# Two block sums of w2 made in DRAM by transfers, low sums on VectorE, and a wide seventh product

## The chip, the cores and the metric

The kernel runs on one core of a Trainium2 chip. The metric is the device time of one execution in microseconds (us); the time before is the median of three runs. The engines are named as in the profile: PE is TensorE (PEld its weight loads), DVE is VectorE, ACT is ScalarE, POOL is GpSimd and SP is SyncE, which here only issues transfers. L12 is line 12 of the kernel.

## The reference

The reference is one block with two residual parts, in float32. The input x has 2048 tokens of 512 channels.

```python
x = A_x                                       # (1, 2048, 512)
h = x + A_ref(layernorm(x), wqkv, w_phi, wo)  # linear attention, 32 heads of 16
h2 = h + B_ref(layernorm(h), w1, b1, w2, b2)  # MLP across the tokens
...
# A_ref: pq, pk = q @ w_phi, k @ w_phi;  phi = [softmax(p), softmax(-p)]
#        o = phi_q (phi_k^T v) / (phi_q sum(phi_k) + 1e-6);  o @ wo
# B_ref: u = gelu(h^T w1 + b1)   (512 channels x 2048 tokens, w1 2048 x 1792)
#        y = u w2 + b2           (w2 1792 x 2048), transposed back
```

## The kernel before

Each float32 operand is split into a high part and a low part (`split`: ScalarE copies the high part, VectorE or GpSimd subtracts it for the low part), and a product is made from three matmuls: high by high, high by low, low by high.

The work runs in stages. The first pass (0 to 138 us) makes k, v and q of the 16 token tiles and the sums of the linear attention. In before a scheduler orders the engines in this pass except TensorE, whose order is written out (`PASSES`). From there the order of every engine is written out by hand. The second pass (138 to 263 us) has 18 turns of a loop over `it`: `s_ez` and `s_pq` weight the query features on GpSimd, `s_tr` transposes them on TensorE, `s_num` and `s_wo` make the attention output, `s_h` adds it to x, `s_moments`, `s_rstd` and `s_hn` make the layernorm, and `fill` makes the first products with w1 (weights `whl`, loaded by `stream`). Then come the steps with w1 (263 to 372 us) and the steps with w2 (372 to 511 us).

The w2 steps (kind "y") use a seven-product scheme for 2 x 2 blocks. There are 8 block columns `sp` of 256 tokens and 7 steps `p` in each. In one step, `load_raw` puts four 128 x 128 blocks of w2 into slots 1 to 4 of a tile of seven (`wraw`), one transfer per step on SP's queue. Four sums complete them. `w_sums` makes these on VectorE for four steps at once (L793 to L797):

```python
nc.vector.tensor_add(raw[:, :, 0], raw[:, :, 3], raw[:, :, 1])   # L793
nc.vector.tensor_add(raw[:, :, 5], raw[:, :, 0], raw[:, :, 2])   # L794
nc.vector.tensor_add(raw[:, :, 6], raw[:, :, 4], raw[:, :, 5])   # L795
nc.vector.tensor_add(raw[:, :, 1], raw[:, :, 1], raw[:, :, 2])   # L797
```

`w_parts` splits the seven blocks into `wp` (L66 on ScalarE, L67 on VectorE). `prepare` calls both several steps ahead of the products. `wide_step` makes the seven products P1 to P7 in the first seven block columns, `last_step` in the eighth. A product is either `narrow` (three matmuls of 256 columns, L951) or `wide` (one of 512 columns with the high and low part of u side by side, L958, and one of 256 columns with the low weights, L960). A wide product fills both halves of its PSUM bank: the second half holds the sum of high by low, which must be added in the end. Before, P2 to P5 are wide and P1, P6, P7 narrow. The banks are b16 (P1 and P6), b7, b5, b4, b3 and b2. At the end of a block column ScalarE and VectorE combine the banks into four output tiles and add b2, and `store` sends them by adding transfers on GpSimd's queue (L1001) into the output, which holds h. Four stores per block column are made, two of 128 x 512 and two of 128 x 256: the low sums of P4 and of P3 and P2 go as stores of their own.

For the "u" steps with w1, `add_raw` makes sums in the same tile by adding transfers on GpSimd's queue (L783), 128 rows of 1 KB each.

Of the kernel before, what the change touches and what calls it, by code (L numbers as in the profile page):

```python
# [17 lines left out]
P = 128  # L18
# [5 lines left out]
NPR = 2 * NG  # L24
Q_EARLY = 6

PASSES = [(s[0], int(s[1:] or 0)) for s in
          "k5 v f k6 v q k7 q v k8 v q v q k9 k10 v k11 q k12 v k13 v q k14 v".split()]
PKS = 8
SUMS = 8  # L30
Q_TURNS = ((0, 1), (0, 1), (0, 1), (0, 1), (0,), (1,), (0,), (1,))
# [11 lines left out]
def block_kernel(ctx: ExitStack, tc: tile.TileContext, x, xT, wT, phic, wo, w1, b1, w2, b2,  # L43
# [2 lines left out]

    cst = ctx.enter_context(tc.tile_pool(name="cst", bufs=1))
    big = ctx.enter_context(tc.tile_pool(name="big", bufs=NT + 2))

    ident = cst.tile([P, P], F32, name="ident")  # L50
    mask = cst.tile([P, 64], F32, name="mask")
# [62 lines left out]
    def load_h(t):  # L114
        XH[t] = kk.tile([P, D], F32, name="xh", bufs=3)
        nc.sync.dma_start(XH[t], x[t * P:(t + 1) * P, :])

    def split_x(t, raw, alone=False):
# [4 lines left out]
        else:  # L123
            split(X[t][:, 0], X[t][:, 1], raw, nc.gpsimd)

    def stats_x(t):
        junk = kk.tile([P, D], F32, name="sqj", bufs=1)
        st = kk.tile([P, 2], F32, name="st")
        nc.scalar.activation(junk, XH[t], AF.Copy, scale=-1.0 / D, accum_out=st[:, 0:1])
        nc.scalar.activation(junk, XH[t], AF.Square, bias=st[:, 0:1], accum_out=st[:, 1:2])  # L130
        ve = kk.tile([P, 1], F32, name="ve")
        nc.vector.tensor_scalar(ve, st[:, 1:2], 1.0 / D, EPS, op0=ALU.mult, op1=ALU.add)
        nc.gpsimd.tensor_tensor(r1[:, t:t + 1], ve, mhalf[:, :1], op=ALU.pow)

    def proj(t, wh, wl, pool, name, by_part=False, halves=1):
        o = pool.tile([P, D], F32, name=name, tag=name)
# [24 lines left out]
    def logit_ops(src, e, pool):  # L161

        v = src.rearrange("p (j h d) -> p j h d", h=2, d=DH)
        ev = signs(e)
        mx = wk.tile([P, NPR, 2], F32, name="mx")
        mn = wk.tile([P, NPR, 2], F32, name="mn")

        def shift():
            nc.vector.tensor_sub(ev[:, :, 0], v, mx.unsqueeze(3).to_broadcast([P, NPR, 2, DH]))
            if pool:  # L170
                MN.append((ev, mx, mn))
            else:
# [17 lines left out]
    def run(*lists):  # L190
        for op in turns(*lists):
            op()

    def exps(t, e):
        nc.scalar.activation(e, e, AF.Exp, scale=r1[:, t:t + 1])  # L195

    def heads(e):
        return e.rearrange("p g (a d) -> p (g a) d", d=DH)

    def k_ops(t, o):  # L200
        PK[t] = kk.tile([P, NG, P], F32, name="pk", bufs=PKS)
        run(logit_ops(o, PK[t], False))

    def k_logits(t):
        k_ops(t, proj(t, wkh, wkl, ps_k, "pk_ps"))
        exps(t, PK[t])

    def v_out(t, o):
        VS[t] = kk.tile([P, D], F32, name="vs", bufs=5)
        nc.scalar.activation(VS[t], o, AF.Copy, scale=r1[:, t:t + 1])  # L210

    def v_proj(t):
        v_out(t, proj(t, wvh, wvl, ps_v, "pv"))

    def k_norm(t, z=True):
        sk = wk.tile([P, 2 * H], F32, name="sk", bufs=2)
        nc.vector.reduce_sum(sk, heads(PK[t]), axis=AX.X)
        nc.vector.reciprocal(sk, sk)  # L218
        nc.gpsimd.tensor_mul(heads(PK[t]), heads(PK[t]), sk.unsqueeze(2).to_broadcast([P, 2 * H, DH]))  # L219
        if z and t == 0:  # L220
            nc.gpsimd.tensor_copy(zacc, PK[t])
        elif z:
            nc.gpsimd.tensor_add(zacc, zacc, PK[t])  # L223
# [57 lines left out]
    with tc.tile_pool(name="prep", bufs=1) as prep:  # L281
# [77 lines left out]
        with tc.manual_schedule(engines={ET.PE, ET.DVE, ET.Activation, ET.Pool}):  # L359
# [61 lines left out]
            lo_w(0)  # L421
            lo_w(1)
            center(3, False)
        stats_x(3)
        exps(3, PK[3])
        load_h(4)
        stats_x(4)
        k_ops(4, k4)
        exps(4, PK[4])
        v_out(2, v2)  # L430

        def fold_rest():
            for c in range(2, 4):
                fold(c, ps_q, "pu")
                hi_w(c)
                lo_w(c)

        def k_step(t):

            if t + 2 < NT:  # L440
                raw = load_x(t + 2)
                load_h(t + 2)
            if t > 4:
                k_logits(t)
            k_norm(t - 1)
            if t + 2 < NT:
                split_x(t + 2, raw)
                stats_x(t + 2)

        def q_step(_):  # L450
            q_mm()
            run(q_logits(0))
            q_exp(0)
            run(q_sums(0))


        with tc.manual_schedule(engines={ET.PE}):
            k_step(3)
            k_step(4)
            for name, n in PASSES:  # L460
                {"k": k_step, "v": lambda _: v_kv(), "q": q_step, "f": lambda _: fold_rest()}[name](n)

    ms = ExitStack()
    ms.enter_context(tc.manual_schedule(engines={ET.PE, ET.DVE, ET.Activation, ET.Pool, ET.SP}))
# [86 lines left out]
    proj_part(pv, v, wvh, wvl, range(1, KD))  # L551
    v_out(v, pv)
    v += 1
    s_ez(0)
    s_ez(1)
    run(s_den(0, ps_d, "dn"))
# [108 lines left out]
            nc.scalar.activation(HN[t][:, 0], hn, AF.Copy)  # L665
            DL.append(lambda: nc.vector.tensor_sub(HN[t][:, 1], hn, HN[t][:, 0]))

    w1v = w1.rearrange("(k p) f -> p k f", p=P)
    w2v = w2.rearrange("(k p) s -> p k s", p=P)

    COMING, LATER = [], []

    def his():
# [85 lines left out]
    def load_raw(g):  # L759
        if 2 * g >= len(STEPS):  # L760
            return
        b = g // 2 % 2
        if b not in BLOCK:
            BLOCK[b] = cbb.tile([P, 4, 7, P], F32, name="wraw") if b else wqp.tile([P, 4, 7, P], F32, name="wraw", tag="wq")
        RAW[g] = BLOCK[b][:, g % 2 * 2:g % 2 * 2 + 2]
        for k in range(2):
            src, r, c = blocks(2 * g + k)
# [18 lines left out]
    def w_sums(g):  # L786

        if 2 * g >= len(STEPS) or STEPS[2 * g][0] == "v":
            return
        plain = STEPS[2 * g][0] == "y"  # L790
        raw = BLOCK[g // 2 % 2] if plain else RAW[g]
        if plain:
            nc.vector.tensor_add(raw[:, :, 0], raw[:, :, 3], raw[:, :, 1])  # L793
# [35 lines left out]
    for it in range(NT + 2):  # L829
        if it < NT:  # L830
            s_x(it)
        shifted = q["logits"] - len(MN)
        ql = q_logits(0)
        work = turn(it)
# [168 lines left out]
    def wide_step(n, sp, p):  # L1003
# [7 lines left out]
        def x(m):  # L1011
            return UB[p, m]
# [1 line left out]
        def ws_(*products):  # L1014
            wide(n, x, first, end, *products)

        w3, w2, w5, w4 = (b3, P3), (b2, P2), (b5, P5), (b4, P4)
# [12 lines left out]
        ws_(w3, w2)  # L1030
        tmp, ot, lows = [ur.tile([P, 4, HD], F32, name="u") for _ in range(3)]
# [8 lines left out]
        sub(u2, b16[:, 1], e1)  # L1040
# [4 lines left out]
        add(l5, b5[:, 0], l5)  # L1045
        add(e0, l5, u2)
        nc.scalar.activation(lows[:, 0], b3[:, 1], AF.Copy)  # L1047
        nc.scalar.activation(lows[:, 1], b2[:, 1], AF.Copy)
        tile_sum(0, 0, l5, u3)
        tile_sum(1, 0, b3[:, 0], e0, ALU.subtract)  # L1050
        tile_sum(1, 1, b2[:, 0], e1)
        return [(t, 1, lows[:, 3:4]), (t, 0, ot[:, 0:2]), (t + 1, 0, ot[:, 2:4]), (t + 1, 0, lows[:, 0:2])]

    def last_step(n, sp, p):
        t = 2 * sp
# [93 lines left out]
        at(n, u_parts, p)  # L1149
    at(len(STEPS) - 18, last_h, NT - 2)  # L1150
    at(len(STEPS) - 12, last_b, NT - 2)
    HB = []
    load_raw(2)
    load_raw(3)
# [103 lines left out]
```

## Time and profile before

| | before |
|---|---|
| median of 3 runs | 517.14 us (516.28 to 517.21) |
| the profiled execution | 516.23 us, its span 514.454 us |
| granted TensorE clock | 1.000 |
| PE busy | 509.4 us, 99% of the span |
| DVE, ACT, POOL busy | 432.5, 300.7, 247.1 us (84%, 58%, 48%) |
| chain that ended last | PE 95%, DVE 2%, ACT 1% |
| bytes moved | 61.76 MB, mean 120 GB/s |

The span is what the trace covers; the rest of an execution's time lies around it. A share of busy time is a mean over stages with different limits. Matmul times in the rows are times in flight, and the matmuls overlap. A row of the timeline reads: start, duration, engine, line, operation, output<-input, shapes, count, and in brackets the idle time before it and what ended that. A row of groups ends with busy time, mean ns of one, and idle time with its releasers. A row of windows has the busy time of PE, PEld, DVE, ACT and POOL with their counts, then the granted clock, the share of the DMA engines and GB/s.

### The profile page before, as it was taken

What the parts mean: (1) busy time and instruction counts of PE and PEld (TensorE: products, weight loads), DVE (VectorE), ACT (ScalarE), POOL (GpSimd) and SP (SyncE); (2) the same over time, 40 slices, a digit from 0 to 9 for tenths busy, and PEclk for the clock granted to TensorE, in tenths of its full rate; (3) what the DMA queues carried; (4) which work ended last, traced back from release to release, by engine and by line L of the source; (5) the groups of instructions that cost most, each with busy time, mean ns of one, the idle gap of its engine ahead of it and who ended that gap; (6) DMA issues with size and microseconds to landing.
All of it is one profiled execution on the core that took longest, in us unless ns stands there. A gap on an engine that the chain in (4) does not pass through costs nothing.

```text
span 514.5 us, 10292 instructions
## 1 busy us (share of the span) xinstructions
PE 509.4 (99%) x3954; PEld 439.7 (85%) x3954; DVE 432.5 (84%) x736; ACT 300.7 (58%) x530; POOL 247.1 (48%) x195
## 2 busy tenths in 40 slices
PE   9999999999999999999999999999999999999997
PEld 8888888888877777777788999988899999999997
DVE  6799889989887899699876878986789989968973
ACT  6999853526267878867675636555364434434530
POOL 3579997876999999975203330000002112211220
PEclk9999999999999999999999999999999999999999
DMA  8642301020113233443329784333425687668743
GB/s 306 218 143 84 103 22 42 1 77 8 43 62 103 81 104 126 147 160 126 103 79 256 152 194 120 103 103 102 143 63 126 162 194 172 128 152 192 168 63 71
DMA packets 52112, 61.76 MB, mean 120 GB/s; under 512 B 4704, under 2 KB 38752, under 8 KB 52064
## 3 DMA queue, kind: packets, MB, share of 16 engines
q1 hardware_dynamic: 45440, 52.43, 32.6%
q0 software_dynamic: 6336, 8.52, 12.1%
q8 instruction: 31, 0.51, 0.4%
q10 hardware_dynamic: 288, 0.17, 0.1%
q14 instruction: 17, 0.14, 0.1%
HBM read 49.96 MB, written 11.14 MB: 119 GB/s over the span
## 4 chain that ended last, share of the span: by engine, by line
PE 95%; DVE 2%; ACT 1%; issue 0%; DVEq 0%
PE py L951 22%; PE pu L71 10%; PE pu L72 9%; PE pu L73 9%; PE py L958 9%; PE py L960 4%; PE pk_ps L71 3%; PE pk_ps L72 3%; PE pk_ps L73 3%; PE pv L73 3%; PE pv L72 3%; PE pv L71 3%; PE po L71 3%; PE po L73 2%; PE po L72 2%; PE pn L616 2%
## 5 line engine op out<-in xcount | busy, mean ns | idle before, releaser
L66 ACT ACTIVATE wp<-wraw 128x896 fp32r<-128x896 f32 (+1 forms) x96 | 79.8, 869 | 83.4 <-DVE wraw L797 34.1
L67 DVE TENSOR_TENSOR wp<-wraw,wp 128x896 fp32r<-128x896 f32 (+1 forms) x96 | 92.3, 986 | 20.7 <-ACT wp L66 20.5
L1001 POOL DMA_DIRECT2D out<-u x28 | 24.5, 952 | 170.0 <-ACT u L1047 110.8
L951 PE MATMUL py<-cb,wp 128*128 128x256 f32 x582 | 79.8, 283 | 0.0
L951 PEld LDWEIGHTS py<-cb,wp 128*128 128x128 f32 x582 | 74.0, 191 | 0.0
L490 POOL TENSOR_TENSOR ez<-eq,zB 128x1024 f32<-128x1024 f32 x16 | 38.4, 2404 | 3.8 <-ACT zB L550 3.8
L71 PE MATMUL pu<-hs,wp 128*128 128x512 f32 x96 | 37.4, 389 | 0.0
L72 PE MATMUL pu<-hs,wp 128*128 128x512 f32 x96 | 37.4, 389 | 0.0
L73 PE MATMUL pu<-hs,wp 128*128 128x512 f32 x96 | 37.3, 389 | 0.0
L219 POOL TENSOR_TENSOR pk<-pk,sk 128x1024 f32<-128x1024 f32 x16 | 31.1, 1943 | 11.3 <-DVE sk L218 10.1
L958 PE MATMUL py<-cb,wp 128*128 128x512 f32 x126 | 36.1, 394 | 0.0
L514 POOL TENSOR_TENSOR eq<-eq,w 128x1024 f32<-128x1024 f32 x16 | 32.4, 2026 | 3.5 <-DVE w L511 3.5
L223 POOL TENSOR_TENSOR zacc<-zacc,pk 128x1024 f32<-128x1024 f32 x13 | 31.3, 2406 | 0.5
L783 POOL DMA_DIRECT2D wraw<-in_w x16 | 14.2, 970 | 31.7 <-DMA wraw<-in_w 21.3
L195 ACT ACTIVATE pk<-pk,r 128x1024 f32<-128x1024 f32 x16 | 18.4, 1148 | 15.0 <-DVE pk L173 14.4
L951 PE MATMUL py<-uf,wp 128*128 128x256 f32 x198 | 26.6, 283 | 0.0
L71 PE MATMUL pu<-wq,xs 128*128 128x512 f32 x64 | 26.1, 408 | 0.0
L71 PE MATMUL pu<-hs,whl 128*128 128x512 f32 x64 | 26.0, 406 | 0.0
L71 PE MATMUL po<-woh,oh 128*128 128x512 f32 x64 | 25.3, 395 | 0.1
L72 PE MATMUL pu<-wq,xs 128*128 128x512 f32 x64 | 25.0, 391 | 0.0
L72 PE MATMUL pu<-hs,whl 128*128 128x512 f32 x64 | 25.0, 390 | 0.0
L73 PE MATMUL po<-woh,ol 128*128 128x512 f32 x64 | 25.0, 390 | 0.0
(213 smaller groups left out, 1398.5 us busy)
## 6 DMA issues: line engine op xcount, KB each, us to landing
wraw<-in_w SPq DMA_DIRECT2D x112, 256.0 KB, 3.4
out<-u POOLq DMA_DIRECT2D x21, 256.0 KB, 5.2
xraw<-in_xT SPq DMA_DIRECT2D x16, 256.0 KB, 3.0
xh<-in_x SPq DMA_DIRECT2D x16, 256.0 KB, 2.6
h<-in_x SPq DMA_DIRECT2D x16, 256.0 KB, 2.8
out<-h SPq DMA_DIRECT2D x16, 256.0 KB, 2.0
wraw<-in_wT SPq DMA_DIRECT2D x12, 256.0 KB, 5.2
wraw<-in_w POOLq DMA_DIRECT2D x16, 128.0 KB, 3.9
```

The costliest lines, as they stand in the source:

```text
L66: nc.scalar.activation(hi, src, AF.Copy)
L67: lo_engine.tensor_sub(lo, src, hi)
L71: nc.tensor.matmul(o, ah, bh, start=first, stop=False)
L72: nc.tensor.matmul(o, ah, bl, start=False, stop=False)
L73: return nc.tensor.matmul(o, al, bh, start=False, stop=last).ins
L219: nc.gpsimd.tensor_mul(heads(PK[t]), heads(PK[t]), sk.unsqueeze(2).to_broadcast([P, 2 * H, DH]))
L223: nc.gpsimd.tensor_add(zacc, zacc, PK[t])
L490: nc.gpsimd.tensor_mul(EZ[t], EQ[t], zB)
L514: nc.gpsimd.tensor_mul(heads(EQ[t]), heads(EQ[t]), W[t].rearrange("p g c h -> p (g c h)").unsqueeze(2).to_broadcast([P, 2 * H, DH]))
L951: nc.tensor.matmul(o, w[:, m[0]], x[:, y], start=opens and i == 0, stop=closes and i == 2, skip_group_check=True)
L958: nc.tensor.matmul(o, wh_[:, m[0]], x(m[1]), start=first, stop=False, skip_group_check=True)
L1001: nc.gpsimd.dma_start(out[t * P:(t + 1) * P, k * HD:], flat(a), accum_op=ALU.add)
```

## The change

Slots 0 and 1 of a w2 step (the sums of L793 and L797) are made in DRAM. A new DRAM tile `w2s` per block column holds both for all seven steps. `copy_w2(n)` copies one of the two summands on ScalarE's queue, 16 copies of 896 rows of 512 bytes; `add_w2(sp)` adds the other summands by one adding transfer on GpSimd's queue, 8 of 896 rows of 1 KB. The first pass now follows a written order for all engines (`FIRST`), which is the order that the scheduler gave before, with twelve copies and four adds put into it. Adds 4 and 5 stand before the first `s_ez`, adds 6 and 7 in turns 15 and 16 of the second pass, and four copies in its turns 2 to 8. `load_raw` of a w2 step has three transfers: the two sums, one block alone, and two blocks. `w_sums` loses two of its four adds.

In `wide_step` P7 becomes wide. At the end of a block column ScalarE copies one low sum more, VectorE adds the four low sums (four operations more), and two stores of 128 x 512 remain. TensorE's order is otherwise that of before: the built program has 3353 matmuls where it had 3402, 49 fewer.

```diff
+    def copy_w2(n):
+        sp, k = divmod(n, 2)
+        if k == 0:
+            W2S[sp] = dram.tile([P, NP, 2, P], F32, name=f"w2s{sp}")
+        src = w2v.rearrange("p (j i) s -> p j i s", i=2)
+        nc.scalar.dma_start(W2S[sp][:, :, k], src[:, :, 1 - k, 2 * sp * P:2 * sp * P + P])
+
+    def add_w2(sp):
+        src = w2v.rearrange("p (j i) s -> p j i s", i=2)
+        nc.gpsimd.dma_start(W2S[sp].rearrange("p j k s -> p j (k s)"), src[:, :, 0, 2 * sp * P:2 * sp * P + 2 * P],
+                            accum_op=ALU.add)
...
+        with tc.manual_schedule(engines={ET.PE, ET.DVE, ET.Activation, ET.Pool, ET.SP}):
+            for token in FIRST.split():
+                DO[token[0]](int(token[1:]))
...
     v_out(v, pv)
     v += 1
+    add_w2(4)
+    add_w2(5)
     s_ez(0)
...
+            if kind == "y":
+                nc.sync.dma_start(RAW[g][:, k, 0:2], W2S[i][:, j])
+                nc.sync.dma_start(RAW[g][:, k, 2], src[:, r, c + P:c + 2 * P])
+                nc.sync.dma_start(RAW[g][:, k, 3:5].rearrange("p i s -> p (i s)"), src[:, r + 1, c:c + 2 * P])
+                continue
...
-        if plain:
-            nc.vector.tensor_add(raw[:, :, 0], raw[:, :, 3], raw[:, :, 1])
         nc.vector.tensor_add(raw[:, :, 5], raw[:, :, 0], raw[:, :, 2])
         nc.vector.tensor_add(raw[:, :, 6], raw[:, :, 4], raw[:, :, 5])
-        if plain:
-            nc.vector.tensor_add(raw[:, :, 1], raw[:, :, 1], raw[:, :, 2])
...
+        for n in {2: (12,), 4: (13,), 6: (14,), 8: (15,)}.get(it, ()):
+            copy_w2(n)
...
+        if it in {15: 6, 16: 7}:
+            add_w2({15: 6, 16: 7}[it])
...
-            ws_(w3, w2, w5, w4)
+            ws_(w3, w2, w5, w4, w7)
         narrow(b16[:, 0], n, P1, x(1), first, end)
         narrow(b16[:, 1], n, P6, x(5), False, end)
-        narrow(b7[:, 0], n, P7, x(0), first, end)
         if first:
-            ws_(w5, w4)
+            ws_(w7, w5, w4)
         if not end:
             return []
+        ws_(w7)
         ws_(w4, w5)
         ws_(w3, w2)
...
-        nc.scalar.activation(e1, b16[:, 0], AF.Copy)
+        l7, l3, l2, l4 = lows[:, 3], lows[:, 0], lows[:, 1], ot[:, 1]
+        for o, bank in ((e1, b16), (l7, b7), (l5, b5), (l4, b4)):
+            nc.scalar.activation(o, bank[:, int(o is not e1)], AF.Copy)
         sub(u2, b16[:, 1], e1)
         sub(u3, u2, b7[:, 0])
-        nc.scalar.activation(l5, b5[:, 1], AF.Copy)
-        nc.scalar.activation(lows[:, 3], b4[:, 1], AF.Copy)
-        tile_sum(0, 1, b4[:, 0], u3)
         add(l5, b5[:, 0], l5)
+        sub(u3, u3, l7)
+        add(l4, b4[:, 0], l4)
         add(e0, l5, u2)
-        nc.scalar.activation(lows[:, 0], b3[:, 1], AF.Copy)
-        nc.scalar.activation(lows[:, 1], b2[:, 1], AF.Copy)
+        nc.scalar.activation(l3, b3[:, 1], AF.Copy)
+        nc.scalar.activation(l2, b2[:, 1], AF.Copy)
+        tile_sum(0, 1, l4, u3)
         tile_sum(0, 0, l5, u3)
-        tile_sum(1, 0, b3[:, 0], e0, ALU.subtract)
-        tile_sum(1, 1, b2[:, 0], e1)
-        return [(t, 1, lows[:, 3:4]), (t, 0, ot[:, 0:2]), (t + 1, 0, ot[:, 2:4]), (t + 1, 0, lows[:, 0:2])]
+        add(l3, b3[:, 0], l3)
+        add(l2, b2[:, 0], l2)
+        tile_sum(1, 0, l3, e0, ALU.subtract)
+        tile_sum(1, 1, l2, e1)
+        return [(t, 0, ot[:, 0:2]), (t + 1, 0, ot[:, 2:4])]
```

More of the change, by code (lines that the diff above doesn't have):

```diff
@@ L25 @@
 Q_EARLY = 6
-PASSES = [(s[0], int(s[1:] or 0)) for s in
-          "k5 v f k6 v q k7 q v k8 v q v q k9 k10 v k11 q k12 v k13 v q k14 v".split()]
+FIRST = """
+X5 H4 X6 a5 X7 b5 a6 b6 H5 X8 X9 s3 a7 S3 b7 a8 H6 X10 u3 b8 l4 r3 s4 m4 n2 k5 S4 C0 o2 H7 X11 x4 y4 s5 N2 v3
+u4 p2 e3 l5 r4 S5 m5 F2 H8 n3 s6 F3 x5 e4 k6 u5 C1 y5 r5 S6 N3 o3 H9 n4 p3 c2 v4 u6 s7 N4 c3 d2 z2 e5 d3 l6 S7
+C2 K0 m6 K1 H10 r6 s8 n5 K2 p4 S8 K3 o4 H11 q0 x6 u7 y6 s9 C3 z3 u8 e6 N5 k7 S9 n6 H12 s10 r7 N6 r8 S10 u9 p5
+H13 s11 C4 u10 f0 q1 S11 g0 H14 h0 s12 z4 a9 i0 S12 C5 l7 v5 E0 H15 m7 p6 x7 j0 k8 r9 y7 r10 f1 e7 b9 g1 a10
+u11 u12 z5 X12 h1 v6 s13 C6 i1 o5 n7 S13 E1 r11 N7 r12 q2 u13 l8 s14 C7 b10 m8 S14 j1 z6 X13 s15 S15 v7 x8 o6
+y8 p7 u14 e8 C8 q3 o7 n8 r13 r14 f2 z7 g2 k9 u15 N8 h2 i2 r15 p8 f3 E2 C9 k10 g3 a11 C10 j2 a12 z8 a13 C11 h3
+v8 i3 l9 E3 b11 m9 x9 X14 b12 K4 y9 K5 j3 e9 X15 b13 A0 A1 K6 K7 k11 o8 l10 m10 n9 q4 x10 y10 N9 e10 p9 n10
+k12 N10 z9 l11 m11 v9 x11 p10 y11 f4 e11 g4 k13 a14 z10 h4 a15 i4 n11 E4 b14 v10 o9 l12 m12 b15 N11 j4 p11 q5
+x12 y12 z11 l13 e12 k14 m13 x13 y13 n12 e13 v11 o10 N12 n13 p12 f5 g5 z12 N13 h5 i5 p13 l14 E5 m14 o11 x14 z13
+A2 A3 y14 j5 e14
+"""
 PKS = 8
@@ L124, in split_x, with stats_sum, stats_square, stats_var @@
             split(X[t][:, 0], X[t][:, 1], raw, nc.gpsimd)
-    def stats_x(t):
[L127 to L133, printed above, removed]
+    def stats_sum(t):
+        junk = kk.tile([P, D], F32, name="sqj", bufs=1)
+        ST[t] = kk.tile([P, 2], F32, name="st")
+        nc.scalar.activation(junk, XH[t], AF.Copy, scale=-1.0 / D, accum_out=ST[t][:, 0:1])
+    def stats_square(t):
+        junk = kk.tile([P, D], F32, name="sqj", bufs=1)
+        nc.scalar.activation(junk, XH[t], AF.Square, bias=ST[t][:, 0:1], accum_out=ST[t][:, 1:2])
+    def stats_var(t):
+        ST[t], st = kk.tile([P, 1], F32, name="ve"), ST[t]
+        nc.vector.tensor_scalar(ST[t], st[:, 1:2], 1.0 / D, EPS, op0=ALU.mult, op1=ALU.add)
+    def stats_rstd(t):
+        nc.gpsimd.tensor_tensor(r1[:, t:t + 1], ST[t], mhalf[:, :1], op=ALU.pow)
+    def stats_x(t):
+        for f in (stats_sum, stats_square, stats_var, stats_rstd):
+            f(t)
     def proj(t, wh, wl, pool, name, by_part=False, halves=1):
@@ L198, in heads, with logit_list @@
         return e.rearrange("p g (a d) -> p (g a) d", d=DH)
+    def logit_list(t, o):
+        PK[t] = kk.tile([P, NG, P], F32, name="pk", bufs=PKS)
+        return logit_ops(o, PK[t], False)
     def k_ops(t, o):
[L201 to L206, printed above, removed]
+        run(logit_list(t, o))
     def v_out(t, o):
@@ L213, in v_proj, with norm_sum, norm_rec, norm_mul @@
         v_out(t, proj(t, wvh, wvl, ps_v, "pv"))
-    def k_norm(t, z=True):
[L216 to L223, printed above, removed]
+    def norm_sum(t):
+        SK[t] = wk.tile([P, 2 * H], F32, name="sk", bufs=2)
+        nc.vector.reduce_sum(SK[t], heads(PK[t]), axis=AX.X)
+    def norm_rec(t):
+        nc.vector.reciprocal(SK[t], SK[t])
+    def norm_mul(t):
+        nc.gpsimd.tensor_mul(heads(PK[t]), heads(PK[t]), SK[t].unsqueeze(2).to_broadcast([P, 2 * H, DH]))
+    def norm_z(t):
+        if t == 0:
+            nc.gpsimd.tensor_copy(zacc, PK[t])
+        else:
+            nc.gpsimd.tensor_add(zacc, zacc, PK[t])
+    def k_norm(t, z=True):
+        norm_sum(t)
+        norm_rec(t)
+        norm_mul(t)
+        if z:
+            norm_z(t)
     def kv(t):
@@ L423, in block_kernel @@
             center(3, False)
[L424 to L448, printed above, removed]
@@ L450, in q_step, with k_mm @@
-        def q_step(_):
-            q_mm()
[L452 to L461, printed above, removed]
+        LO_K, LO_Q, PV = {4: logit_list(4, k4)}, {}, {2: v2}
+        def k_mm(t):
+            LO_K[t] = logit_list(t, proj(t, wkh, wkl, ps_k, "pk_ps"))
@@ new lines, in v_mm, with q_list, hi_x @@
+        def v_mm(t):
+            PV[t] = proj(t, wvh, wvl, ps_v, "pv")
+        def q_list(n):
+            q_mm()
+            EQ[n] = big.tile([P, NG, P], F32, name="eq", tag="big")
+            LO_Q[n] = logit_ops(PS[n], EQ[n], False)
+        def hi_x(t):
+            X[t] = big.tile([P, 2, KD, P], F32R, name="xs", tag="big")
+            nc.scalar.activation(X[t][:, 0], xr[t], AF.Copy)
+        DO = {
+            "X": lambda t: xr.update({t: load_x(t)}), "H": load_h,
+            "a": hi_x, "b": lambda t: nc.gpsimd.tensor_sub(X[t][:, 1], xr[t], X[t][:, 0]),
+            "s": stats_sum, "S": stats_square, "u": stats_var, "r": stats_rstd,
+            "k": k_mm, "l": lambda t: LO_K[t][0](), "m": lambda t: LO_K[t][1](),
+            "x": lambda t: LO_K[t][2](), "y": lambda t: LO_K[t][3](), "e": lambda t: exps(t, PK[t]),
+            "n": norm_sum, "N": norm_rec, "p": norm_mul, "z": norm_z,
+            "v": v_mm, "o": lambda t: v_out(t, PV[t]), "K": kv,
+            "C": copy_w2, "A": add_w2, "q": q_list, "f": lambda t: LO_Q[t][0](), "g": lambda t: LO_Q[t][1](),
+            "h": lambda t: LO_Q[t][2](), "i": lambda t: LO_Q[t][3](), "E": lambda t: exps(t, EQ[t]),
+            "j": lambda t: run(q_sum(t)), "F": lambda c: fold(c, ps_q, "pu"), "c": hi_w, "d": lo_w,
+        }
@@ L1151, in block_kernel @@
     at(len(STEPS) - 12, last_b, NT - 2)
+    for sp, n in ():
+        at(n, add_w2, sp)
     HB = []
```

19 lines of the change are left out of this document (12 added, 7 removed).

## The prediction

> **What bounds the kernel now.** I read the page first, for its engine shares and the chain that ended last, then TensorE's waits.
>
> ```profile
> span 514.5 us, 10292 instructions
> PE 509.4 (99%) x3954; PEld 439.7 (85%) x3954; DVE 432.5 (84%) x736; ACT 300.7 (58%) x530; POOL 247.1 (48%) x195
> ...
> DMA  8642301020113233443329784333425687668743
> ...
> q1 hardware_dynamic: 45440, 52.43, 32.6%
> q0 software_dynamic: 6336, 8.52, 12.1%
> ...
> PE 95%; DVE 2%; ACT 1%; issue 0%; DVEq 0%
> ```
> ```profile
> PE pk_ps L358 <- DVE eps L62: 1.1, 1, 1.1
> PE pn L616 <- DVE h L641: 0.2, 1, 0.2
> PE pu L336 <- POOL ph L361: 0.2, 1, 0.2
> ```
>
> TensorE (PE) holds 95% of the chain and waits 1.5 us in all, 1.1 of it at the start. So only two things move the time: fewer TensorE cycles, or a new wait of TensorE. Work taken from VectorE, or from the stores on GpSimd (POOL), is worth nothing by itself. The profiled execution took 516.23 us, 1.7 outside its 514.5 span, and lies 0.91 below the median of 517.14. I sum differences against that execution and add them to the median. A difference within 0.2%, 1.03 us, can't be told from none here.
>
> **TensorE's saving.** Forty-nine times (seven block columns by seven steps) the seventh product turns from three 256-column matmuls into one of 512 and one of 256. The chain in order of time prices both forms, inside one w2 step:
>
> ```profile
> 393.41 1.08 PE py L951 x9
> 394.49 0.93 PE py L958 x4
> 395.42 0.47 PE py L960 x4
> ```
>
> Nine narrow ones in 1.08 are 0.120 each, the wide ones 0.2325, their low halves 0.1175. Three narrow are 0.360; one wide and one low 0.350. The saving is 0.010 x 49 = 0.49 us. The rows of groups seem to promise more:
>
> ```profile
> L951 PE MATMUL py<-cb,wp 128*128 128x256 f32 x390 | 54.1, 282 | 0.0
> ...
> L958 PE MATMUL py<-cb,wp 128*128 128x512 f32 x126 | 36.1, 394 | 0.0
> ...
> L960 PE MATMUL py<-cb,wp 128*128 128x256 f32 x126 | 21.5, 279 | 0.0
> ```
>
> 3 x 282 against 394 + 279 would be 173 ns, 8.5 us over 49. But these are times in flight, of matmuls that overlap: 282 ns each, started every 120. I take the chain.
>
> **Adding transfers on GpSimd.** Eight are issued, each 896 rows of 1 KB, DRAM to DRAM, which the trace does not show. Nearest are the adding transfers for w1 of 128 such rows, and the gaps where the new ones stand (two after the low part of x, at 85.36 - 3.17 = 82.2, two before the one at 114.64, two before the first ez at 126.79, one before the rstd at 255.60, one behind it):
>
> ```profile
> L783 POOL DMA_DIRECT2D wraw<-in_w x16: 858/870/1223, 273.4 to 308.8; - x16
> ```
> ```profile
> 85.36 1.94 POOL L219 TENSOR_TENSOR pk<-pk,sk 128x1024 f32<-128x1024 f32 x1 [3.17 <-DVE sk L218]
> ...
> 102.24 1.94 POOL L219 TENSOR_TENSOR pk<-pk,sk 128x1024 f32<-128x1024 f32 x1 [1.20 <-ACT vs L210]
> ...
> 114.64 1.94 POOL L219 TENSOR_TENSOR pk<-pk,sk 128x1024 f32<-128x1024 f32 x1 [3.61 <-DVE sk L218]
> ...
> 126.79 4.75 POOL L490 TENSOR_TENSOR ez<-eq,zB 128x1024 f32<-128x1024 f32 x2 [3.82 <-ACT zB L550]
> ...
> 137.61 1.94 POOL L514 TENSOR_TENSOR eq<-eq,w 128x1024 f32<-128x1024 f32 x1
> ...
> 255.60 0.55 POOL L652 TENSOR_TENSOR r<-ve,mhalf 128x1 f32<-128x1 f32 x1 [2.42 <-ACT ve L649]
> ```
> ```profile
> 142.53 0.28 PE L598 MATMUL tr<-ident,eq 64*128 64x64 f32 x2
> ```
> ```profile
> 131.00:220.00 89.00, 88.78 (x982) 69.74 (x981) 75.82 (x155) 64.43 (x126) 87.00 (x64) 1.00 0.31 101
> ```
>
> Let one issue cost a: at least 0.87 (the median), at most seven times that, 6.1. The three pairs make GpSimd late by max(0, 2a - 3.17); that, less 1.2 of idle time between (the row at 102.2), plus 2a - 3.61; that plus 2a - 3.82. Behind the last pair stand ez and the weighting of the queries (L514), with GpSimd full until 220 (87.00 of 89.00 us in the window), so lateness stays. TensorE takes the second weighting's result at 142.53, and it ends at 139.55, so 3.0 us are covered. At a = 2.0 the pairs end 0.6 late at most, at 2.5 about 3.2, which costs TensorE 0.15 us; from there each 0.1 costs about 0.6. The point of decision is a = 2.5 (2.7 for a loss that can be measured). The gap of 2.42 at 255.60 asks about the same. I take a = 1.5, an estimate nearer the low end: half of the 16 issues lie between 858 and 870 ns, so constant that most of it looks like a fixed part. Price nothing, cover 3.0.
>
> [...] No row here shows more than 128 rows.
>
> **Copies on ScalarE (ACT).** Sixteen of 896 rows of 512 B. A 128-row load occupies its queue 0.34 to 0.43 us (SP's rows below); seven times the larger is 3.0. I take 0.6, since the issue is by hardware and a load of twice as many rows costs little more. Where ScalarE has no idle time to spare, two copies precede the last weights of q:
>
> ```profile
> 43.86 1.22 DVE L354 TENSOR_TENSOR wq<-pu,wq 128x512 fp32r<-128x512 f32 x2
> ```
> ```profile
> 49.15 0.50 PE L71 MATMUL pu<-wq,xs 128*128 128x512 f32 x1
> ```
>
> VectorE is done at 45.08, TensorE asks at 49.15: 4.1 us cover for 1.2; at 3.0 each, 6.0 would cost 1.9. Later copies stand further ahead of what TensorE asks for, the last four where ScalarE waits for VectorE. Price nothing, bound 1.9.
>
> **Packets of the new transfers.** q0's mean packet costs 0.121 x 16 x 514.5 / 6336 = 157 ns, q1's 59. An adding transfer is then 896 x 157 / 16 = 8.8 us of all 16 engines; by bytes, 0.92 of 8.52 MB, it is 6.7. In the first pass the DMA engines are mostly free. Not so for the two at 253 and 256:
>
> ```profile
> 254.53 0.43 SPq L691 DMA_DIRECT2D wraw<-in_w  x1
> ```
> ```profile
> 257.89 0.62 ACT L677 ACTIVATE whl<-wraw 128x512 fp32r<-128x512 f32 x1
> ```
> ```profile
> 258.54 0.69 DVE L684 TENSOR_TENSOR whl<-wraw,whl 128x512 fp32r<-128x512 f32 x1 [1.81 <-ACT whl L677]
> ...
> 260.35 0.68 DVE L666 TENSOR_TENSOR hs<-hf,hs 128x512 fp32r<-128x512 f32 x1
> ```
> ```profile
> 261.25 0.40 PE L72 MATMUL pu<-hs,whl 128*128 128x512 f32 x1
> ```
>
> The w1 load issued at 254.53 is used by ScalarE at 257.89; VectorE waits for that, does two parts, then the low part of hs, done at 261.03 for a matmul at 261.25: 0.2 us of slack. How long that load and the w1 loads from 265 to 300 take from issue to landing:
>
> ```profile
> DMA to landing us min/median/max: 2.8/2.8/2.8
> ```
> ```profile
> DMA to landing us min/median/max: 2.7/3.7/4.9
> ```
>
> It lands at 257.3 and lies 0.6 us before ScalarE is free. The sixth add's packets run from about 255 on and share the engines with it. The later loads share them with adds for w1 and take up to 4.9, so this one comes 0 to 2.1 late, and TensorE stalls by what exceeds 0.8: 0 to 1.3. I take 1.0 late, 0.2 stalled. The seventh add falls on the loads of the w1 steps, before a stretch already full:
>
> ```profile
> 260.00:265.00 5.00, 5.00 (x24) 4.10 (x23) 4.39 (x10) 3.22 (x8) 0.64 (x1) 1.00 0.14 52
> 265.00:270.00 5.00, 5.00 (x24) 4.14 (x23) 3.88 (x5) 4.34 (x7) 0.00 (x0) 1.00 0.50 145
> 270.00:275.00 5.00, 5.00 (x24) 4.14 (x23) 2.39 (x3) 1.14 (x3) 1.56 (x2) 1.00 1.07 355
> ```
>
> From 263 to 270 about 4.2 of 7 us are free, for 6.7 to 8.8: a backlog of 2.5 to 4.6 us behind 270. VectorE idles 4.3 of the 15 us from 260 to 275 (15 less 4.39, 3.88 and 2.39), which absorbs about all of it. I take nothing; the larger backlog against half of that idle time leaves 2.4, my bound.
>
> **The w2 steps.** VectorE loses two adds per four steps and gains four small operations per block; GpSimd's stores go from four to two; a step's load becomes three. Rows:
>
> ```profile
> L793 DVE TENSOR_TENSOR wraw<-wraw 128x512 f32<-128x512 f32 x13 | 8.9, 687 | 5.8 <-DMA wraw<-in_w 5.2 <-DVE wp L67 0.6
> ```
> ```profile
> 389.06 0.42 DVE L1040 TENSOR_TENSOR u<-py,u 128x256 f32<-128x256 f32 x1
> ...
> 390.55 0.41 DVE L1045 TENSOR_TENSOR u<-py,u 128x256 f32<-128x256 f32 x1
> ```
> ```profile
> 389.39 0.63 PE L958 MATMUL py<-cb,wp 128*128 128x512 f32 x2
> ```
>
> Per block VectorE sheds 3.5 x 0.69 = 2.4 and gains 4 x 0.42 = 1.7 us. Two more issues of 0.43 land a load 0.9 later; VectorE already waits 5.2 us for loads here (L793's row) and TensorE does not notice, so 0.9 is covered. What is new is when the banks of b5 and b4 come free: b4's after five operations, not three. At their spacing of 0.50, from 389.06, the fifth ends at 391.47. TensorE wants that bank 1.88 after the block's start at 389.39 (two wide and two low products 0.70, six narrow 0.72, two wide 0.47): 391.27. That is 0.2 late for a start like this one; VectorE, with 0.7 us less per block, starts earlier. Price 0.0, bound 7 x 0.2 = 1.4.
>
> **Sum.** -0.49 + 0.2 = -0.3: 515.9 for the profiled execution, 516.85 on the median, told as 516.9.
>
> **Rivals.**
> *GpSimd's issues cost more than 2.5 us* (slower). By rows in place of transfers, a may be anything to 6.1. At 3.0 the stall is 3.2 us, giving 519.8; at 3.5, 6.2 and 522.8; at 6.1, some 22 and 538. Against it: the flat 0.87. The rows' own spread, 858 to 1223, shows that an issue can be held by others. [...] Chance 0.20, a tenth of all beyond 523.
> *The load at 254.53 comes late and the seventh add holds the w1 loads too* (slower): it decides from 2.4 late on (1.6 stalled, less 0.5 saved). With both bounds, 1.3 + 2.4 = 3.7 stalled, 518.2 to 520.4. For it: the 0.2 slack, and windows with the DMA full. Against it: the load is nearly through when the add's packets come. Chance 0.15.
> *The w2 steps lose their cover* (slower): banks 0.2 to 0.4 late in seven blocks and three small loads for one: 1.5 to 2.8 stalled, 518.2 to 519.5. Chance 0.10.
> *TensorE gains more than the chain says* (faster): if a narrow product's weight load were what paces it, one start of 0.120 fewer each would be 5.9 us, 511.3; by the rows in flight, 508.7. Against it: wide and low products already run in these steps at 0.35 together. A smaller gain, just below 516.1, would come if the seventh product's saving were twice the chain's. That the change does not do what it says is no case: the built program holds 49 matmuls fewer. Chance 0.15.
>
> **How the numbers follow.** Forecast 0.40, within 1.03 of the median before: same 0.40. The three slower rivals sum to 0.45, the faster one to 0.15. The forecast's own range is 516.6 (no stall) to 518.2 (1.5 stalled, where the slower rivals begin). The range given, 515.8 to 523.0, leaves out about a tenth at each end.
>
> **What would show it.** Right: TensorE still with 95% of the chain and the seventh product's pair at 0.35 us; the new issues on GpSimd under 2.5 us each, ez at 126.8, the whl row near 258 and no wait of TensorE above 1 us after the first. Wrong: issue rows of several us and ez past 130; a TensorE wait for hs near 261; waits for banks at block starts; or w2 steps well under 2.46 us.

## The result and the profile after

The changed kernel takes 548.9 us (548.35 to 550.31, five runs) against 516.52 before (516.28 to 517.21, five runs): a ratio of 1.0625 [1.0607, 1.0643]. It is 32 us slower. The forecast was 516.9, in a range up to 523.0. GpSimd's issues were among the rivals, but as too dear in themselves, which they are not, and a time beyond 523 had a chance of a tenth. Adds and copies are numbered from 0 here, as in the change: add 6 is the one that the prediction calls the sixth.

The page of after, profiled in an execution of 548.96 us:

```profile
span 547.2 us, 10409 instructions
...
PE 518.9 (95%) x3905; PEld 443.2 (81%) x3905; DVE 423.1 (77%) x736; ACT 303.2 (55%) x537; POOL 245.9 (45%) x189
...
PEclk9999999997779999999997999999999999999999
...
PE 47%; DVE 3%; DMA 2%; issue 1%; ACT 0%; SPq 0%; DVEq 0%
...
w2s<-in_w ACTq DMA_DIRECT2D x16, 448.0 KB, 5.0
w2s<-in_w POOLq DMA_DIRECT2D x8, 896.0 KB, 9.8
```

TensorE is 9.5 us longer busy with 49 matmuls fewer, and its granted clock falls in two places. Its waits in after, longest first:

```profile
PE pk_ps L595 <- ACT zh L580: 11.6, 1, 11.6
PE pu L98 <- ACT whl L723: 3.1, 1, 3.1
PE tr L647 <- POOL eq L561: 3.0, 1, 3.0
PE pu L98 <- DVE eq L207: 2.4, 1, 2.4
PE pu L99 <- DVE hs L715: 2.0, 1, 2.0
PE pk_ps L409 <- DVE eps L89: 1.1, 1, 1.1
PE pk_ps L596 <- DVE zl L583: 0.6, 1, 0.6
PE po L98 <- DVE ol L674: 0.4, 1, 0.4
```

TensorE's order is the same in both programs up to the w2 steps, so the same matmul can be looked up in both. In before:

```profile
124.97 0.39 PE L548 MATMUL pk_ps<-zh,ones_r 128*128 128x512 f32 x1
...
141.94 0.67 PE L616 MATMUL pn<-pht,small 64*32 64x128 f32 x32
...
263.75 0.39 PE L71 MATMUL pu<-hs,wp 128*128 128x512 f32 x1
```

And in after:

```profile
137.77 0.80 PE L595 MATMUL pk_ps<-zh,ones_r 128*128 128x512 f32 x1 [11.62 <-ACT zh L580]
...
166.25 0.54 PE L665 MATMUL pn<-pht,small 64*32 64x128 f32 x14
...
296.28 0.39 PE L98 MATMUL pu<-hs,wp 128*128 128x512 f32 x1
```

After is 12.8 us behind at the first, 24.3 at the second and 32.5 at the third, and 32.7 at the end of the span. All but the first 1.0 (by 105 us) arises in two places: from 125 to 166 us, and around the last w1 load of the second pass. The w2 steps add nothing and take nothing.

GpSimd's timeline in after shows the first place:

```profile
82.93 1.64 POOL L74 DMA_DIRECT2D w2s<-in_w  x1
92.84 1.49 POOL L74 DMA_DIRECT2D w2s<-in_w  x1 [8.27 <-DVE eq L207]
93.61 2.69 POOL L261 TENSOR_TENSOR pk<-pk,sk 128x1024 f32<-128x1024 f32 x1
...
118.69 1.49 POOL L74 DMA_DIRECT2D w2s<-in_w  x1
128.55 1.49 POOL L74 DMA_DIRECT2D w2s<-in_w  x1 [8.36 <-issue]
129.29 2.71 POOL L261 TENSOR_TENSOR pk<-pk,sk 128x1024 f32<-128x1024 f32 x1
132.08 2.34 POOL L567 TENSOR_TENSOR zacc<-zacc,pk 128x1024 f32<-128x1024 f32 x1
...
138.53 1.51 POOL L74 DMA_DIRECT2D w2s<-in_w  x1 [0.56 <-issue]
148.18 1.48 POOL L74 DMA_DIRECT2D w2s<-in_w  x1 [8.13 <-issue]
148.92 3.15 POOL L537 TENSOR_TENSOR ez<-eq,zB 128x1024 f32<-128x1024 f32 x1
```

An issue itself takes 1.5 us, just what I took for a. But the second of a pair starts 9.6 to 9.9 us after the first, which is how long an add takes to land (9.8 in the page). In the trace's DMA events the first of each pair landed at 92.58, 128.23 and 147.86, and the second starts 0.3 us after that. GpSimd stands idle for 8 us in between. The name behind the arrow does not tell the cause: "DVE eq" ended at 92.59, but an add from DRAM to DRAM reads nothing of it, and the other two have "issue" there. What GpSimd does next is late: the last part of the sum z (132.08, in before 116.66), then `zh`, for which TensorE waits 11.6 us, then ez (148.92, in before 126.79). The row of z in before:

```profile
116.66 2.73 POOL L520 TENSOR_TENSOR zacc<-zacc,pk 128x1024 f32<-128x1024 f32 x1
```

### The profile page after: what moved, and what is told of

Its sections match the earlier page's. It is cut to its first block, busy times and chain, and to the rows that moved or that the text cites. A ratio compares the mean times of both kernels' runs of the same rounds, so it can differ in the third digit from the quotient of the medians.

```text
span 547.2 us, 10409 instructions
## 1 busy us (share of the span) xinstructions
PE 518.9 (95%) x3905; PEld 443.2 (81%) x3905; DVE 423.1 (77%) x736; ACT 303.2 (55%) x537; POOL 245.9 (45%) x189
## 4 chain that ended last, share of the span: by engine, by line
PE 47%; DVE 3%; DMA 2%; issue 1%; ACT 0%; SPq 0%; DVEq 0%
PE py L1003 17%; PE py L1010 10%; PE py L1012 5%; PE pu L99 5%; PE pu L100 5%; PE pu L98 5%; DMA wraw<-in_w 2%; DVE u L785 1%; DVE whl L730 1%; DVE u L784 0%; DVE ol L674 0%; PE po L98 0%; DVE tr L550 0%; DVE wp L94 0%; ACT pht L649 0%
## 5 line engine op out<-in xcount | busy, mean ns | idle before, releaser
L1053 POOL DMA_DIRECT2D out<-u x14 | 12.0, 859 | 177.6 <-DVE u L1104 173.4
L1003 PE MATMUL py<-cb,wp 128*128 128x256 f32 x477 | 66.1, 283 | 0.0
L1003 PEld LDWEIGHTS py<-cb,wp 128*128 128x128 f32 x477 | 61.1, 192 | 0.0
L1010 PE MATMUL py<-cb,wp 128*128 128x512 f32 x161 | 45.3, 394 | 0.0
L261 POOL TENSOR_TENSOR pk<-pk,sk 128x1024 f32<-128x1024 f32 x16 | 32.6, 2039 | 3.4 <-DVE sk L258 3.4
L1010 PEld LDWEIGHTS py<-cb,wp 128*128 128x128 f32 x161 | 27.6, 189 | 3.4
L98 PE MATMUL pu<-hs,whl 128*128 128x512 f32 x64 | 26.8, 418 | 3.1 <-ACT whl L723 3.1
L98 PE MATMUL pu<-wq,xs 128*128 128x512 f32 x64 | 27.2, 425 | 2.4 <-DVE eq L207 2.4
L1012 PEld LDWEIGHTS py<-cb,wp 128*128 128x128 f32 x161 | 25.4, 189 | 3.6
L99 PE MATMUL pu<-hs,whl 128*128 128x512 f32 x64 | 26.1, 408 | 2.0 <-DVE hs L715 2.0
L234 ACT ACTIVATE eq<-eq,r 128x1024 f32<-128x1024 f32 x16 | 18.4, 1150 | 17.2 <-DVE eq L212 8.9
L74 POOL DMA_DIRECT2D w2s<-in_w x8 | 12.1, 1518 | 34.1 <-issue 25.9
```

What stands on the lines that cost most here:

```text
L98: nc.tensor.matmul(o, ah, bh, start=first, stop=False)
L99: nc.tensor.matmul(o, ah, bl, start=False, stop=False)
L261: nc.gpsimd.tensor_mul(heads(PK[t]), heads(PK[t]), SK[t].unsqueeze(2).to_broadcast([P, 2 * H, DH]))
L1003: nc.tensor.matmul(o, w[:, m[0]], x[:, y], start=opens and i == 0, stop=closes and i == 2, skip_group_check=True)
L1010: nc.tensor.matmul(o, wh_[:, m[0]], x(m[1]), start=first, stop=False, skip_group_check=True)
L1012: nc.tensor.matmul(o[:, 0], wl_[:, m[0]], x(m[1])[:, 0], start=False, stop=last, skip_group_check=True)
```

## The experiments

**The changed kernel without the adds.** The first question was whether anything else costs.

```diff
     def add_w2(sp):
-        src = w2v.rearrange("p (j i) s -> p j i s", i=2)
-        nc.gpsimd.dma_start(W2S[sp].rearrange("p j k s -> p j (k s)"), src[:, :, 0, 2 * sp * P:2 * sp * P + 2 * P],
-                            accum_op=ALU.add)
+        return
```

> The changed kernel without its eight adding transfers (the two block sums in DRAM lack one summand, so the output is wrong); copies, DRAM loads, the wide seventh product and the low sums stay. Theory A (all 32 us come from the adds: 24.4 from GpSimd's late ez, 7.9 from the w1 load that the sixth add holds): 516.4 to 516.8, no TensorE wait above 1.2 us, and w2 block columns of 17.29 us. Rival (the copies, the small loads or the low sums cost part of it): 518 or more, with waits in the first pass or the w2 steps.

517.19 us, ratio 1.0012 [1.0004, 1.0021]: 0.6 us over before. TensorE waits 1.1 us at the start and 0.2 once more, as before. So copies, small loads and low sums are all but hidden, and all but 0.6 of the 32 us is the adds. That is 0.4 above the range expected. In the profiled execution TensorE starts its last matmul only 0.15 us later than in before (510.86 against 510.71 us) and the span ends 1.4 later, so the excess lies behind TensorE's work; what makes it was not looked into.

**Twice the scratch space.** The program sets the size of a scratch space for transfers, `dynamic_dma_scratch_size`, 2048 in before and after. I took it for the place where GpSimd keeps the descriptors of its transfers, which say what is to be moved; no trace shows that, and the runs show only what the size does.

```diff
-        dynamic_dma_scratch_size=2048
+        dynamic_dma_scratch_size=4096
-        junk = ak.tile([P, D], F32, name="hj", bufs=1)
+        junk = ak.tile([P, D], mybir.dt.bfloat16, name="hj", bufs=1)
-    cst.tile([P, 80], F32, name="pad")
-    wqp.tile([P, 120], F32, name="pad")
```

> The changed kernel with the space for GpSimd's transfer descriptors doubled, from 2048 to 4096 bytes per partition (paid for by a bfloat16 scratch tile and two unused pads). Theory A (the second add of a pair waits because the first one's descriptors fill the ring, until it has landed): the two issues of a pair stand 1.5 us apart, not 9.9; ez at 127 to 129; the 24.4 us vanish, the 7.9 around the w1 load stay: 523 to 526. Rival B (a large add waits until the one before has landed whatever the space): issues 9.9 us apart and 548 to 550. Rival C (the descriptors of 896 rows take GpSimd itself 10 us): the same as B.

GpSimd's timeline of this kernel:

```profile
83.50 3.14 POOL L74 DMA_DIRECT2D w2s<-in_w  x2
...
113.89 3.02 POOL L74 DMA_DIRECT2D w2s<-in_w  x2
...
126.51 1.52 POOL L74 DMA_DIRECT2D w2s<-in_w  x1 [0.32 <-issue]
132.03 1.48 POOL L74 DMA_DIRECT2D w2s<-in_w  x1 [4.00 <-issue]
```

The first two pairs go out in 3.1 and 3.0 us without a wait. Add 4 then starts 0.3 us after add 2 has landed (126.19 in the trace's DMA events), add 5 0.3 us after add 3 has (131.73). With 2048 bytes one add was in flight at a time (the second of a pair started 9.6 to 9.9 us after the first), with 4096 two were. The issues go as theory A has it, though what fills the space was not shown; rivals B and C fall: neither knows why the space should matter. The expectation missed in two points all the same. ez starts at 132.8, not 127 to 129, because the last pair still waits, and near 144 TensorE waits 1.8 us for `eq`, as it did in after (2.4). And the time, 534.6, is above my 523 to 526 for two more reasons: the kernel without pads is slower by itself (below), and now both later adds are in flight beside the w1 load, where TensorE waits 3.8 and 2.0 us.

**Adds of 384 rows.**

```diff
-        nc.gpsimd.dma_start(W2S[sp].rearrange("p j k s -> p j (k s)"), src[:, :, 0, 2 * sp * P:2 * sp * P + 2 * P],
+        nc.gpsimd.dma_start(W2S[sp][:, 0:3].rearrange("p j k s -> p j (k s)"), src[:, 0:3, 0, 2 * sp * P:2 * sp * P + 2 * P],
                             accum_op=ALU.add)
```

> The changed kernel with adds of three steps of the seven in each block column: 384 rows, not 896 (the sums of the other four steps lack a summand, so the output is wrong). [...] Rival B (each large add waits for the one before): issues of a pair about 4.5 us apart, ez some 3 us late, 520 to 525.

```profile
82.52 2.70 POOL L74 DMA_DIRECT2D w2s<-in_w  x2
85.81 1.93 POOL L261 TENSOR_TENSOR pk<-pk,sk 128x1024 f32<-128x1024 f32 x1 [0.60 <-DVE sk L258]
```

Two adds of 384 rows go out back to back in 2.7 us, and GpSimd is ready in time; nothing of the 24 us is left. The first alone takes 1.3 us to issue, against 0.87 for 128 rows and 1.5 for 896. The time is 521.3, ratio 1.0096 [1.0070, 1.0122], higher than my 518 to 520. I had estimated a landing of 5.5 us for the w1 load, from 2.8 in before, 9.0 beside an add of 896 rows, and 3/7 of the rows. It still takes 6.6, and TensorE waits 0.7 and 2.0 us; but it falls behind by 6.0 us there in the profiled execution, because its granted clock is 0.50 from 264.2 to 271.0. Two of the four executions, with a mean granted clock of 1.000, took 519.9; the two with 0.992 and 0.997 took 523.8 and 522.7. The load's row here, in after, and without adds, in that order:

```profile
DMA to landing us min/median/max: 6.6/6.6/6.6
```
```profile
DMA to landing us min/median/max: 9.0/9.0/9.0
```
```profile
DMA to landing us min/median/max: 2.9/2.9/2.9
```

**The last two adds moved.**

```diff
-        if it in {15: 6, 16: 7}:
-            add_w2({15: 6, 16: 7}[it])
...
-    for sp, n in ():
+    for sp, n in ((6, 18), (7, 30)):
         at(n, add_w2, sp)
```

> The changed kernel with the sixth and seventh of the adds 0 to 7 moved from the second pass to after steps 18 and 30 of the w1 steps; the three pairs in the first pass stay. Theory A (two separate places: 24.4 us before 145 us, 7.9 at the w1 load near 280): the second goes, the first stays: 540.5 to 542, with the load there landing in about 2.8 us. Rival (the second place is a consequence of the first, whose lateness has used up all slack): 546 or more.

541.07 us, 7.8 below after and as expected: the two places are separate, and the second is the load that add 6 holds. In after that place reads, on ScalarE, then on TensorE:

```profile
288.23 0.63 ACT L723 ACTIVATE whl<-wraw 128x512 fp32r<-128x512 f32 x1 [5.54 <-DMA wraw<-in_w]
```
```profile
288.91 0.49 PE L98 MATMUL pu<-hs,whl 128*128 128x512 f32 x1 [3.07 <-ACT whl L723]
291.45 0.80 PE L99 MATMUL pu<-hs,whl 128*128 128x512 f32 x1 [2.04 <-DVE hs L715]
292.04 0.63 PE L100 MATMUL pu<-hs,whl 128*128 128x512 f32 x1
292.47 0.63 PE L98 MATMUL pu<-hs,whl 128*128 128x512 f32 x1
```

**The adds one at a time.** Three in the first pass, five in the w1 steps, 11 to 13 us apart.

```diff
-... b13 A0 A1 K6 ...
+... b13 A0 K6 ...
...
-A2 A3 y14 ...
+A1 y14 ...
...
-    add_w2(4)
-    add_w2(5)
+    add_w2(2)
...
-    for sp, n in ():
+    for sp, n in ((3, 17), (4, 22), (5, 28), (6, 33), (7, 38)):
```

> The changed kernel with its eight adds one at a time: one each at three of the places in the first pass (after the low part of x, before the weighting near 114, before the first ez), the others after steps 17, 22, 28, 33 and 38 of the w1 steps, where GpSimd has nothing to do. Theory A (waiting for the ring and the load behind the sixth add are all): each issue takes 1.5 us in gaps of 3.2 to 3.8, nothing waits, w1 loads lie 20 us ahead: 516.3 to 517.0, the same as before. Rival (adds slow the w1 loads wherever they stand): TensorE waits in the w1 steps of 2 us or more, 519 to 530.

519.0 us, ratio 1.0054 [1.0035, 1.0073]: above the expectation, and not by its rival's wait in the w1 steps. In the profile TensorE reaches the w2 steps no later than in before (371.94 us against 372.09), so the three adds of the first pass and the w1 steps' loads cost it nothing. But the adds are one at a time only because each still waits: in the w1 steps every one after the first starts 0.3 to 0.4 us after the one before has landed, 10.9 to 12.4 us after its issue. This costs TensorE nothing by itself, but it pushes the last add back until it lands at 371.60. The first two block columns then take 18.5 and 18.7 us, not 17.3: the adds issued at 348.45 and 360.56 stand beside the first w2 loads, and VectorE waits for these.

```profile
DVE wraw L843 <- DMA wraw<-in_w: 9.9, 2, 7.8
```

**Three more placements**, so that the last add lands before the w2 loads: five adds in the first pass (at 57, 69, 89, 117 and 128 us, then at 48, 65, 87, 116 and 126, then at 47, 65, 85, 115 and 125), three after steps 17, 22 and 27. Of the edit, only the line of the w1 steps, against the version above:

```diff
-    for sp, n in ((3, 17), (4, 22), (5, 28), (6, 33), (7, 38)):
+    for sp, n in ((5, 17), (6, 22), (7, 27)):
```

> The changed kernel with the eight adds one at a time, at least 10 us apart, five in the first pass (behind two of the running sums of z near 64 and 74, after the low part of x, near 111, before the first ez) and three after steps 17, 22 and 27 of the w1 steps, so that the last has landed before the first w2 loads. Theory A: nothing waits and the block columns take 17.29: as without adds, 517.0 to 517.6. Rival (any add costs something wherever it is): 518 or more.

> The changed kernel with the adds one at a time and at least 12 us apart, since single ones landed after 9.5 to 12.5 us, not 10: behind the sum of z near 48, behind a low part of x near 61, after the low part of x at 82, near 111, before the first ez, and after steps 17, 22 and 27 of the w1 steps. Theory A (adds cost only where one waits for the one before or stands beside a load with little slack): no wait of TensorE above 1.2 us, block columns of 17.29, 516.8 to 517.6, not to be told from the kernel before. Rival (1.5 us of GpSimd per add is too much in the first pass, which the earlier try with its stall near 84 could not separate): 518 or more with a stall near 84.

> As the kernel with the second add near 61, but with that add behind the sum of z near 74: the first add landed only 15.5 us after its issue, so the second waited for it, and GpSimd was 5.1 us late where TensorE covers 4.2. Theory A (adds cost only where one waits for the one before, or where GpSimd's lateness exceeds the cover, or beside tight loads): GpSimd 3.1 late near 80, no stall near 84, 516.6 to 517.4. Rival (any two adds before 82 cost TensorE something): a stall of 0.5 us or more near 84 again, 518 or more.

They took 521.62 (ratio 1.0094 [1.0080, 1.0108]), 519.1 (1.0043 [1.0029, 1.0057]) and 518.97 (1.0040 [1.0026, 1.0054]). All three expectations missed. In each the w2 block columns take 17.29, so the loss at the w2 loads is gone. What remains is a stall of TensorE near 84 us (2.4, 0.7, 0.2 us), by which it falls behind by 4.1, 0.7 and 0.3 us, and near 126 in the last two a wait of 0.3 us, with which it falls behind by 1.0. The 2.4 us cost 4.1 because the granted clock is 0.60 from 86.7 to 91.0. GpSimd in the first of them:

```profile
69.29 1.55 POOL L74 DMA_DIRECT2D w2s<-in_w  x1 [3.67 <-issue]
```

This try did not stand where its expectation has it: its first two adds were put behind the sums of z that run near 55 and 62, not 64 and 74, some 8 us apart, so the second waits for the first. Adds issued at 47 to 48 us landed only 15.0 to 15.5 us later, beside the loads of x and the copies of w2 (25% and 30% of the DMA engines from 47 to 63 us in the second try), so an add placed by a landing time of 10 or 12 us waits again. The last try also stood wrong: behind the sum of z that runs near 62, not near 74, and it reached the queue at 64.6. So neither the first nor the last of the three tests its Theory A. An undisturbed place for a fifth add in the first pass was not found, moving the copies away from the adds was not tried, and no version beat the kernel before.

**The wide product alone**, in the kernel before: its `wide_step` replaced by the new one.

```diff
-            ws_(w3, w2, w5, w4)
+            ws_(w3, w2, w5, w4, w7)
...
-        narrow(b7[:, 0], n, P7, x(0), first, end)
         if first:
-            ws_(w5, w4)
+            ws_(w7, w5, w4)
...
+        ws_(w7)
```

> The kernel before with the new wide_step alone: the seventh product wide, four low sums on VectorE, two stores in place of four; loads and the four adds of the sums as before, nothing in DRAM. By the prediction's step (0.010 us per product) a w2 block column goes from 17.30 to 17.23 us and the time falls by 0.49, to 516.1. Rival, after the changed kernel's 17.29: the matmul time goes by columns, 768 in either form, so 17.29 and no change unless VectorE, with 1.7 us more per block and nothing taken from it, makes TensorE wait: 516.4 to 518.

517.06 us, ratio 1.0005 [0.9996, 1.0014]: no difference, as the rival said. Seven block columns take 121.05 us, in before 121.10, in after 121.05. So the whole gain is 0.05 us, not 0.49. The same place of two block columns that lie four apart, in the chain of before and then of after, shows it (69.20 and 69.17 us):

```profile
407.55 1.07 PE py L951 x9
...
476.75 1.07 PE py L951 x9
```
```profile
407.29 1.15 PE py L1010 x5
...
476.46 1.15 PE py L1010 x5
```

VectorE has 440.6 us of work here and TensorE waits for it no more than in before (1.3 us): the adds that the copies and transfers spare VectorE had not been in TensorE's way.

**Before without its two pads.**

```diff
-    cst.tile([P, 80], F32, name="pad")
-    wqp.tile([P, 120], F32, name="pad")
```

> The kernel before without its two unused pads in SBUF (320 and 480 bytes per partition), which moves the tiles behind them; the kernel with the doubled descriptor space left them out too. If the addresses are why that kernel's TensorE fell behind by a steady 3.6 us up to 131 us and ran its w2 block columns in 17.24 us, this one does likewise: some 521 us before any gain. If not (the larger descriptor space did it), it is the same as before: 516.5.

521.39 us, ratio 1.0090 [1.0075, 1.0105], as expected. TensorE falls behind steadily, 2.7 us by 131, without one wait after the start, and its w2 block columns take 17.24 to 17.32. Near 131 us its 512-column matmuls start every 0.233 us, in before every 0.227. The kernel with the doubled space loses the same: from 10 to 130 us both fall behind by 2.4 us. The other 1.2 of its 3.6 is there by 10 us, where the profiled executions of the other kernels lie between 0.1 us ahead of before and 1.0 behind it. So leaving out the pads explains that loss. The edit changes only where the tiles lie, which makes the addresses the likely cause; how they act was not tried.

## Why the prediction was wrong

*TensorE's saving.* Mis-sized: 0.05 us measured where 0.49 was worked out. I divided merged pieces of the chain by their counts; a piece ends where the next begins, and a boundary of 0.02 in the 1.08 us for nine and of 0.01 in the 1.40 for four pairs is the whole saving. Either form has 768 columns, and the block column is the unit to time: 17.30 against 17.29, 0.353 a product in both. The in-flight means (8.5 us) were rightly left aside.

*Adding transfers on GpSimd.* This is the step that failed. Its price a = 1.5, an estimate between 0.87 and 6.1, came out right (1.48 to 1.64). But the sum made a pair cost 2a, without a reason: it put the wait between the two issues at nothing. In before five adds of 128 rows do go out back to back (273.44 to 278.05), but of two of 896 rows the second starts only when the first has landed (9.6 to 9.9 us apart; with 4096 bytes the first two pairs go out in 3.1 and 3.0 us). A pair costs the landing time of the first plus one issue, 11.4 us (82.93 to 94.33). A number near the landing time stood in the prediction, 8.8 us of packets for one add; it was used for the loads beside the adds and not for GpSimd. With 11.4 in place of 2a the prediction's own sum has ez 22.4 us late and 19.4 stalled; the trace has 22.1 and 17.6. So the chain behind the pairs was right and the price of a pair was not. (At a = 2.5 the sum gives 0.2 us of stall, not 0.15.) The bounds, from rows of issues alone, had 12.2 for a pair at their end, and I gave all beyond 523 us a tenth. Issues took 0.87, 1.3 and 1.5 us for 128, 384 and 896 rows: the cost grew far less than the rows. What makes one issue longer than another of its kind (858 to 1223 ns in before) was not shown; the eight in after lie between 1.48 and 1.64 us.

Of the signs of being wrong that the prediction named, two came, ez past 130 and a wait for hs, but without issue rows of several us: the cost was a wait and not an issue.

*The cover.* I took 3.0 us, from the weighted queries at 142.53. The first reader to be late was another, the sum z at 124.97, which I had not followed, though `zacc` stands among GpSimd's rows. It decides earlier, but with GpSimd 15.4 us late there (132.08 against 116.66) either gives a stall.

*The clock.* Not in the sum at all. The waits above add up to 23.1 us beyond the 1.1 at the start: 17.6 in the first place (11.6, 3.0, 2.4, 0.6), 5.1 in the second (3.1, 2.0) and 0.4 between. The loss is 32.7. Most of the rest is TensorE running slower after each stall, as windows of after show:

```profile
125.00:130.00 5.00, 1.15 (x6) 0.61 (x4) 0.00 (x0) 0.00 (x0) 1.45 (x2) 0.90 0.48 72
130.00:135.00 5.00, 0.00 (x0) 0.00 (x0) 0.00 (x0) 0.00 (x0) 4.92 (x4) 0.50 0.94 114
135.00:140.00 5.00, 1.62 (x3) 0.79 (x3) 3.51 (x5) 2.02 (x3) 4.37 (x4) 0.50 0.47 69
140.00:145.00 5.00, 5.00 (x18) 4.05 (x18) 3.57 (x6) 2.05 (x4) 0.04 (x1) 0.74 0.94 123
145.00:150.00 5.00, 5.00 (x24) 4.14 (x23) 0.00 (x0) 0.67 (x1) 1.82 (x2) 1.00 0.44 64
```

The granted clock falls to 0.50 at about 129 us, some 3 us into the stall, and stays there some 5 us beyond the stall's end at 137.8. Matmuls at that clock start every 0.43 us (292.04 to 292.47, in the second place), not every 0.23. Stalls of 5.1 us cost 7.8 (32.5 less the 24.7 reached before), those of 17.6 cost 23.3 (24.3 less 1.0). In the first of the three placements a wait of 2.4 us was enough for a granted clock of 0.60 (86.7 to 91.0).

*The load at 254.53.* The place and the chain (load, whl, low part of hs, matmul) were right. The landing was mis-sized: 0 to 2.1 us late from loads beside small adds, 6.1 measured (9.0 against 2.9). Beside an add of 896 rows the nearest rows were no bound.

*The copies, the seventh add, the w2 steps.* Right: the copies and the w2 steps cost nothing, within the 0.6 us that the kernel without adds is slower. Add 7 went out only when add 6 had landed, at 289.65; behind it TensorE falls no further behind (32.5 us at 296, 32.6 from 300 on). It was thus not tested where the prediction had it. A copy takes 0.55 to 0.64 us of ScalarE's queue, where I took 0.6. The banks were not waited for.

The forecast's base, that freeing VectorE and the stores is worth nothing here, held. So there was next to no gain to win, and each place of an add could only cost.

## What to carry to other kernels

A transfer issued by GpSimd is priced here by two numbers, the issue (1.5 us) and the time to landing (9.3 us and more), and the second becomes GpSimd's own when the next one has to wait for it, as with 2048 bytes of scratch space (9.6 to 9.9 us from one add to the next) and not for the first two pairs with 4096 (3.1 and 3.0 for both). Ask of a large transfer how many of its kind can be in flight, and place it by its landing time where no load with little slack stands beside it. Stalls of TensorE of 2.4 us and more cost 1.3 to 2.2 times their length here, through the clock (17.6 cost 23.3, 5.1 cost 7.8, 2.4 cost 4.1, and 2.7 in two parts cost 6.0), where one of 0.7 cost 0.7; a saving of a hundredth of a microsecond per matmul has to be read from a whole repeated block, not from a few rows.

## What had not been expected of the hardware

Two unused pads of 320 and 480 bytes per partition are worth 0.9% (516.8 to 521.4 us) of a kernel whose TensorE waits for next to nothing: its steady pace seems to depend on where its tiles lie (0.233 us per matmul against 0.227). Which tiles these are was not tried. An add of 896 KB with no other add in flight landed in 9.3 to 15.5 us, the longest beside other loads and copies, and a load of 256 KB issued 1.4 us after one took 9.0.
